# Sums of squared magnitudes taken on VectorE in every unit, with a new order of the work, in a gated-attention and feed-forward kernel

## The chip, the cores and the metric

The kernel runs on one core of a Trainium2 chip. The metric is the device time of one execution in microseconds; the median of three runs before the change is 659.39 (659.02 to 659.49). Engines are called as the profile calls them: PE (TensorE), PEld (its weight loads), DVE (VectorE), ACT (ScalarE), POOL (GpSimd) and SP (SyncE, which issues the DMAs here).

## The reference

For 4 batches and 8 heads, over 768 positions with head size 48, a complex gate decays a state, and the result goes through a feed-forward block:

```python
mag = np.sqrt(a_re * a_re + a_im * a_im)
scale = np.minimum(mag, 0.999) / (mag + 1e-06)
a_re_n, a_im_n = (a_re * scale, a_im * scale)
for t in range(S):
    new_re = ar * S_re - ai * S_im
    new_im = ar * S_im + ai * S_re
    S_re, S_im = (new_re + k[t] v[t]^T, new_im)
    y[t] = q[t] @ S_re
h = x @ w_in                      # x: y as 3072 tokens of 384; w_in 384 x 2048
sp = np.maximum(h, 0.0) + np.log1p(np.exp(-np.abs(h)))
g = h * erf(sp)
out = g @ w_out                   # 2048 x 384
```

(The state's update is written here in short; ar and ai are the scaled gates at t.)

## The kernel before

**Tiling.** The 3072 tokens are cut into 12 units `u` of 256 tokens, each of two chunks `c` of 128. Three units make up a batch. Within a chunk the recurrence is turned into matrix products: the logarithms of the gates' magnitudes and their angles are summed along time by products with a triangular matrix, keys and queries are multiplied with the decays and the sines and cosines, scores of 128 x 128 are masked, and a state of 96 x 48 per head is carried from chunk to chunk. The feed-forward part works on slabs of eight blocks of 128 columns.

**The order.** Every piece of work is a generator whose `yield`s cut it into steps of about one instruction (or one group of matmuls). A long string, `ORDER` (lines 49 to 168), lists 2,287 tokens; a loop (line 1391) takes them one after the other and runs the next step of the named piece. So `ORDER` fixes the order of instructions in the queue of each engine, SP's DMA queue among them. Each engine works its own queue in order and waits where an operand is not there.

The tokens that this document speaks of: `u` filler products on PE ahead of and between the first real ones; `g`, `k`, `q`, `v` loads; `n`, `i` weights' loads and their conversion, or a second look at them for the check; `m` squared magnitudes (lines 924 to 941), `t` the tangent, `l` logarithms, `r` arctangent, `a` angle sums, `s` sines, `p` decay sums; `K`, `Q` the scaled keys and queries, `A` scores, `S` state, `Y` the attention result; `h` the first feed-forward product, `x` softplus, `e` the erf and its four DVE steps, `f` sums, `O` the second feed-forward product (units 3 and up in seven half-size products, X, Y, Z and W, instead of eight); `Z` the end of the check. `e9.1.4` is unit 9, slab 1, blocks from 4.

**Table loads.** ACT's functions lie in three tables. The helper `act` (line 783) puts a table load in front of a function whose table is not the one loaded last, in the order of the program. Square lies in no table of the helper.

**The check.** The kernel computes by a shorter way that is valid for inputs in some bounds. It collects six sums, among them `large`, per row the sum of the squared magnitudes, compares their totals with limits, and stores one word, `ok` (line 1344). At the end every engine loads `ok` (line 1419) and branches (line 1420): were it 0, a general version of the kernel would follow; it is 1 here. Z has three steps: DVE sums up what was collected (lines 1333 to 1336), PE adds over the rows (line 1339), and DVE compares (lines 1343 and 1344).

**The lines that the change touches.** In unit 0, `g_mag` squares both gate parts on DVE and adds them with an instruction that also writes the row sum. In units 1 to 11 ACT does the squares, the first with the row sum as a second output, and DVE adds.

Of the kernel before, what the change touches and what calls it, by code (L numbers as in the profile page):

```python
# [17 lines left out]
OP = mybir.AluOpType  # L18
# [31 lines left out]
u8_0 u4_38 u4_21 u4_20 u4_2 g0.0 u2_34 u2_41 u2_25 g0.0 g0.1 g0.1 H t0.0 t0.0 m0.0 m0.0 m0.0 m0.1 t0.0 m0.1 l0.0  # L50
l0.0 t0.1 l0.0 l0.0 m0.1 l0.0 t0.1 t0.1 p0.0 u8_1 n0 n0 l0.1 o0.1 l0.1 l0.1 l0.1 o0.0 l0.1 n0 n0 k0.0 q0.0 p0.0
p0.0 K0.0 u2_23 r0.0 a0.0 r0.1 a0.0 a0.0 Q0.0 p0.1 u2_22 a0.1 u2_40 u2_39 g1.0 n1 m1.0 n1 n1 s0.0 s0.0 s0.0 Q0.0
qT0.0.0 p0.1 q0.1 a0.1 t1.0 p0.1 p0.0 K0.0 kT0.0.0 kT0.0.1 qT0.0.1 Q0.1 a0.1 t1.0 qT0.0.0 s0.1 s0.1 s0.1 qT0.0.1
g1.0 kT0.0.0 k0.1 u2_24 v0.0 S0.0 n1 K0.1 kT0.0.1 t1.0 o1.0 r1.0 A0.0.0 A0.0.0 Q0.1 K0.1 p0.0 S0.0 A0.0.1 A0.0.1
n3 n3 g1.1 m1.0 m1.1 t1.1 g1.1 a1.0 m1.0 a1.0 t1.1 a1.0 t1.1 qT0.1.0 qT0.1.0 v0.1 S0.1 S0.1 p0.1 l1.0 n4 n2 m1.1
m1.1 l1.0 g2.0 g2.0 p0.1 kT0.1.1 kT0.1.1 qT0.1.1 qT0.1.1 l1.0 o1.1 l1.0 n3 l1.0 Y0.0 kT0.1.0 A0.1.1 A0.1.1
kT0.1.0 A0.1.0 A0.1.0 l1.1 Y0.0 l1.1 s1.0 l1.1 n3 p1.0 p1.0 q1.0 l1.1 n2 l1.1 n2 g2.1 g2.1 p1.0 p1.0 n5 n6 r1.1
Y0.1 v2.1 k1.0 Y0.1 Q1.0 n2 n4 n4 n4 s1.0 s1.0 Q1.0 p1.1 a1.1 t2 m2 m2 m2 h0.0.6 t2 t2 S0.1 o2 n6 n6 p1.1 h0.0.6
l2 a1.1 a1.1 l2 p1.1 l2 l2 l2 K1.0 K1.0 n7 p1.1 q1.1 n6 k1.1 K1.1 Q1.1 g3.1 h0.0.4 h0.0.4 v1.0 a2.0 r2 a2.0 n7
n7 n7 n5 n5 qT1.0.1 qT1.0.0 h0.0.0 qT1.0.1 h0.0.0 s1.1 qT1.0.0 h0.0.2 h0.0.2 s1.1 s1.1 p2.0 p2.0 kT1.0.1 h0.1.0  # L60
kT1.0.1 kT1.0.0 a2.0 h0.1.0 kT1.0.0 p2.0 x0.0 a2.0 x0.0 e0.0.0 e0.0.2 A1.0.1 A1.0.1 A1.0.0 n5 n8 A1.0.0 n8 a2.0
S1.0 h0.1.6 h0.1.6 q2.0 p1.1 n9 K1.1 S1.0 n8 Q1.1 v1.1 a2.1 a2.1 Q2.0 n8 n9 p1.0 S1.0 Y1.0 Y1.0 qT1.1.1 qT1.1.1
qT1.1.0 qT1.1.0 a2.1 a2.1 a2.1 n9 kT1.1.1 kT1.1.0 n9 S1.1 S1.1 kT1.1.1 kT1.1.0 A1.1.0 A1.1.0 A1.1.1 s2 s2 s2
A1.1.1 S1.1 p2.1 p2.1 Q2.0 k2.0 g3.0 t3 p2.1 m3 t3 K2.0 Q2.0 K2.0 q2.1 Q2.1 K2.0 g3.1 g3.0 t3 v2.0 h0.1.4 Y1.1
Y1.1 n11 n11 k2.1 S2.0 h1.1.0 h0.1.4 m3 p2.0 o3 r3 h0.1.2 m3 l3 h1.1.0 l3 a3.0 a3.0 n10 l3 n11 S2.0 Q2.1 n11
K2.1 n10 l3 a3.0 l3 M2.0 M2.0 M2.0 M2.0 h0.1.2 K2.1 n10 K2.1 n10 g4.0 g4.1 a3.1 g4.1 g4.0 q3.1 h1.0.0 n12 x0.0
x0.0 e0.0.0 e0.0.2 a3.1 e0.0.2 h1.0.2 h1.0.2 p3.0 p3.0 p3.0 p3.1 p3.1 p3.1 k3.0 A2.0.0 e0.0.0 A2.0.1 A2.0.1
e0.0.0 e0.0.2 A2.0.0 e0.0.0 e0.0.2 Q2.1 h1.0.0 m4 a3.1 t4 a3.1 a3.1 m4 t4 e0.0.4 e0.0.4 n12 e0.0.4 t4 e0.0.6
e0.0.6 e0.0.4 e0.0.6 m4 e0.0.6 e0.0.4 n15 k3.1 h1.0.4 h1.0.4 s3 h1.0.6 h1.0.6 Y2.0 p2.0 q3.0 p3.1 n12 e0.0.6
S2.0 n12 M2.1 M2.1 M2.1 M2.1 n13 p3.0 v3.0 s3 p3.0 p3.1 s3 l4 x0.1 Y2.0 l4 x0.1 l4 x0.1 h1.1.6 h1.1.6 x0.1  # L70
e0.1.2 h1.1.2 e0.1.0 h1.1.2 Q3.0 n15 K3.0 Q3.0 l4 Q3.1 o4 n15 K3.0 r4 O0.1 O0.3 O0.0 O0.2 O0.4 O0.6 n15 K3.1
A2.1.0 A2.1.0 A2.1.1 A2.1.1 l4 e0.1.2 e0.1.0 e0.1.2 e0.1.0 h1.1.4 e0.1.2 e0.1.0 e0.1.2 e0.1.0 a4.0 a4.0 n14 Y2.1
v4.1 Y2.1 g5.0 e0.1.6 e0.1.6 e0.1.6 e0.1.4 e0.1.4 e0.1.4 n13 Q3.0 n13 p4.0 O0.5 O0.7 p4.0 a4.0 a4.0 p4.0 a4.0
e0.1.6 e0.1.4 n13 g5.0 a4.1 K3.0 n14 a4.1 e0.1.4 n14 e0.1.6 n14 x1.0 h1.1.4 x1.0 O0.8 h2.1.2 p4.1 O0.9 h2.0.2
O0.11 p4.1 x1.0 p4.1 x1.0 S3.0 S3.0 K3.1 g5.1 g5.1 M3.0 M3.0 M3.0 M3.0 e1.0.0 e1.0.0 e1.0.0 e1.0.2 e1.0.2 h2.0.2
e1.0.0 e1.0.2 e1.0.0 e1.0.2 e1.0.2 h2.1.2 m5 m5 a4.1 a4.1 j m5 O0.13 O0.15 O0.15 e1.0.4 h2.0.6 h2.0.6 e1.0.6
e1.0.6 e1.0.4 e1.0.4 e1.0.4 a4.1 e1.0.6 e1.0.6 e1.0.4 h2.1.4 A3.0.1 K3.1 A3.0.1 Q3.1 e1.0.6 Q3.1 v3.1 A3.0.0 l5
O0.10 A3.0.0 t5 l5 t5 x1.1 l5 l5 x1.1 S3.1 O0.12 O0.14 O0.14 x1.1 h2.0.4 O1.1 O1.3 h2.1.4 Y3.0 t5 S3.1 l5 o5
S3.1 x1.1 l5 l5 e1.1.2 e1.1.0 e1.1.2 e1.1.2 e1.1.2 e1.1.0 e1.1.0 e1.1.2 s4 s4 s4 r5 k4.0 K4.0 e1.1.0 e1.1.0 K4.0
e1.1.6 e1.1.6 e1.1.4 e1.1.4 e1.1.6 e1.1.4 e1.1.6 e1.1.6 O1.5 h2.0.0 O1.0 O1.2 M3.1 M3.1 M3.1 M3.1 A3.1.0 A3.1.0  # L80
A3.1.1 A3.1.1 O1.7 e1.1.4 K4.0 q4.0 Q4.0 k4.1 K4.1 e1.1.4 h2.0.0 h2.0.4 x2.0 Y3.0 x2.0 x2.0 x2.0 v4.0 p4.1 a5.0
p4.0 h2.1.6 O1.9 O1.11 S4.0 Y3.1 h2.1.0 O0.14 a5.0 K4.1 Q4.0 Q4.0 S4.0 q4.1 Q4.1 e2.0.0 e2.0.0 e2.0.0 e2.0.2
e2.0.2 e2.0.2 e2.0.0 e2.0.0 e2.0.2 p5.1 p5.1 h2.1.0 p5.1 e2.0.2 e2.0.6 Y3.1 h2.1.6 e2.0.6 e2.0.6 e2.0.4 a5.0
a5.0 e2.0.4 e2.0.4 O1.4 O1.6 O1.8 O1.13 O1.10 p5.0 p5.0 a5.0 a5.0 a5.0 x2.1 p5.0 x2.1 e2.0.4 e2.0.6 e2.0.6
h3.0.2 p4.0 M4.0 M4.0 M4.0 q5.1 M4.0 O0.15 k5.0 g6.1 p5.0 a5.1 g6.0 a5.1 a5.1 a5.1 x2.1 t6 x2.1 A4.0.1 A4.0.1
S4.1 S4.0 A4.0.0 A4.0.0 K4.1 S4.1 Q4.1 e2.0.4 Q4.1 e2.1.2 e2.1.2 e2.1.2 h3.0.4 h3.0.4 a5.1 O1.12 e2.1.0 e2.1.0
e2.1.2 a5.1 a5.1 e2.1.0 e2.1.2 e2.1.0 e2.1.0 p4.1 k5.1 g6.0 g6.1 h3.0.2 Y4.0 Y4.0 O1.14 O1.14 m6 m6 s5 e2.1.4
O1.15 O1.15 e2.1.6 e2.1.4 e2.1.6 e2.1.4 e2.1.6 h3.0.0 h3.0.0 s5 s5 e2.1.4 e2.1.4 S4.1 m6 e2.1.6 e2.1.6 h3.0.6
h3.0.6 M4.1 M4.1 M4.1 M4.1 h3.1.0 x3.0 t6 h3.1.0 x3.0 l6 x3.0 l6 x3.0 A4.1.1 h3.1.4 O2.1 O2.3 l6 K5.0 K5.0 q5.0
Q5.0 Q5.0 e3.0.0 Q5.0 v5.0 h3.1.6 A4.1.0 S5.0 t6 Q5.1 K5.1 A4.1.1 Q5.1 A4.1.0 Y4.1 K5.0 o6 S5.0 e3.0.0 e3.0.2  # L90
e3.0.0 e3.0.0 e3.0.2 e3.0.2 e3.0.0 e3.0.2 h3.1.4 r6 l6 O2.5 O2.7 a6.0 e3.0.6 a6.0 l6 e3.0.2 h3.1.2 O2.0 h3.1.2
h3.1.6 O2.9 e3.0.4 e3.0.6 e3.0.6 e3.0.4 a6.0 a6.0 O2.2 M5.0 a6.0 e3.0.4 M5.0 M5.0 M5.0 O2.4 O2.6 A5.0.0 A5.0.1
l6 l6 a6.1 p5.0 v6.0 q6.0 e3.0.6 e3.0.6 b2 e3.0.4 x3.1 Y4.1 h4.0.0 x3.1 a6.1 a6.1 x3.1 A5.0.0 A5.0.1 a6.1 a6.1
Y5.0 a6.1 b0 x3.1 O1.14 K5.1 K5.1 S5.0 a6.1 e3.0.4 Y5.0 f3.0 b4 Q5.1 e3.1.0 e3.1.0 e3.1.0 e3.1.0 e3.1.0 e3.1.2
e3.1.2 e3.1.2 e3.1.2 e3.1.2 k6.0 v6.1 O2.11 O2.13 p6.0 p6.0 p6.0 h4.0.0 p6.1 p6.1 e3.1.6 e3.1.6 h4.0.2 h4.0.2
e3.1.4 Q6.0 e3.1.4 O1.15 e3.1.4 e3.1.6 g7.0 g7.0 g7.1 p6.1 K6.0 f3.0 g7.1 m7 m7 M5.1 m7 e3.1.6 e3.1.4 e3.1.6
M5.1 i0 k6.1 i1 p6.0 q6.1 p6.1 M5.1 M5.1 O2.15 h4.0.4 h4.0.4 t7 O2.8 O2.10 O2.15 t7 l7 O2.12 O2.14 O2.14 O2.15
O2.14 b2 b2 t7 b0 b0 i0 l7 s6 l7 l7 b4 l7 b6 b2 e3.1.4 i1 f3.1 b6 b6 b4 h4.0.6 h4.0.6 x4.0 x4.0 b4 f3.1 l7 l7
x4.0 h4.1.0 O3.0 h4.1.0 x4.0 e4.0.0 a7.0 b6 O3.1 e4.0.2 h4.1.6 h4.1.6 o7 O3.1 r7 s6 A5.1.1 A5.1.1 O3.2 O3.2
e4.0.0 e4.0.2 e4.0.0 e4.0.2 e4.0.0 e4.0.2 e4.0.2 b0 e4.0.0 A5.1.0 s6 e4.0.4 e4.0.6 A5.1.0 a7.0 a7.0 e4.0.4  # L100
e4.0.4 e4.0.6 e4.0.6 h4.1.4 h4.1.4 O3.3 O3.4 h4.1.2 O3.5 v5.1 Y5.1 O3.6 O3.7 h4.1.2 x4.1 Y5.1 x4.1 a7.0 e4.0.4
Q6.0 Q6.0 K6.1 e4.0.6 O3.5 O3.5 K6.0 K6.0 O3.5 e4.0.4 Q6.1 O3.4 O3.7 O3.7 p6.1 M6.0 M6.0 e4.0.6 a7.0 a7.0 a7.0
x4.1 x4.1 e4.1.0 e4.1.0 e4.1.0 e4.1.2 p7.1 h5.0.2 h5.0.4 O3.8 O3.9 O3.12 p7.0 O3.10 O3.13 O3.11 p7.1 h5.0.2 p7.1
e4.1.2 e4.1.0 e4.1.2 e4.1.0 e4.1.2 e4.1.2 e4.1.6 e4.1.4 e4.1.6 e4.1.6 e4.1.4 e4.1.4 M6.0 M6.0 a7.1 g8.1 p6.0
a7.1 e4.1.6 e4.1.4 p7.0 h5.0.4 p7.0 a7.1 O3.13 e4.1.6 a7.1 f4.0 e4.1.4 f4.1 O3.11 S6.0 h5.0.6 g8.0 t8 t8 h5.0.6
m8 h5.0.0 Q6.1 i2 i2 A6.0.1 a7.1 a7.1 f4.1 a7.1 S6.0 q7.1 p7.0 i3 A6.0.1 O4.0 O4.1 A6.0.0 O4.2 O4.1 i3 O3.11
h5.0.0 A6.0.0 g8.0 O4.3 p7.1 g8.1 q7.0 O3.13 f4.0 O4.2 t8 o8 Q6.1 K6.1 K6.1 M6.1 M6.1 M6.1 x5.0 x5.0 x5.0 m8
x5.0 O4.4 O4.4 e5.0.2 e5.0.0 e5.0.2 e5.0.0 Q7.0 e5.0.2 e5.0.2 e5.0.0 m8 e5.0.0 e5.0.2 e5.0.0 h5.1.6 h5.1.6 s7 s7
s7 Q7.0 h5.1.2 h5.1.2 e5.0.6 e5.0.6 e5.0.4 e5.0.4 S6.1 e5.0.4 l8 M6.1 v7.0 O4.5 O4.5 S6.1 e5.0.6 h5.1.0 h5.1.4
h5.1.4 l8 h5.1.0 x5.1 Q7.1 S6.1 O4.5 e5.0.6 e5.0.4 O4.5 O4.6 O4.7 Y6.0 O4.7 O4.7 Q7.0 l8 l8 l8 A6.1.1 A6.1.1  # L110
x5.1 Y6.0 A6.1.0 O4.12 O4.13 A6.1.0 O4.8 Q7.1 k7.1 K7.1 v8.0 k7.0 K7.0 K7.0 K7.0 e5.0.4 e5.0.6 x5.1 l8 x5.1 l8
e5.1.0 e5.1.2 e5.1.0 e5.1.2 e5.1.0 e5.1.2 e5.1.0 e5.1.0 e5.1.2 e5.1.2 O4.9 Y6.1 Y6.1 O4.10 O4.11 p8.0 p8.0 p8.0
# [1339 lines left out]
```

## Time and profile before

| | |
|---|---|
| median of three runs | 659.39 us |
| the profiled execution | 659.63 us |
| its span, first to last instruction | 657.9 us |
| granted PE clock, mean | 0.997 |
| PE / PEld / DVE / ACT busy | 642.2 / 562.6 / 599.2 / 581.7 us |
| table loads on ACT | 95, 121.9 us |
| DMA | 70.19 MB, 107 GB/s on average |

In a row of groups, the parts are: line, engine, operation, output and inputs with their shapes, count, busy us and mean ns of one, and after the second bar how long the engine stood idle right before these instructions and what ended most of that. In the table of windows each row has the stretch, its length, then busy us and number of instructions of PE, PEld, DVE, ACT and POOL, the granted clock, the DMA share and GB/s. A row of waits names who waited, for whom, us in total, times, and the longest. The chain of waits is followed back from the last instruction; its rows are start, length and what ran. Matmul ends are modelled and matmuls overlap, so their busy time cannot show short gaps.

### The profile page before, as it was taken

The page shows a single profiled execution, that of the slowest core. Times are in us where ns is not written, and L with a number is a line of the kernel's source. Part 1 is how long each engine was busy: PE and PEld are TensorE (multiplying, and loading weights), DVE is VectorE, ACT ScalarE, POOL GpSimd, SP SyncE. Part 2 cuts the span into 40 slices and gives each one's busy share as a digit, 9 for nine tenths or more (in the row PEclk, how much of TensorE's full clock was granted, in tenths as well). Part 3 has the DMA queues.
Part 4 walks back from the last instruction along what each step waited for, and adds up shares of the span by engine and source line. Part 5 has one row for each costly group of instructions (what it writes and reads, how often), then busy time and mean ns, then how long its engine had stood idle before and what let it go on. Part 6 is the DMA issues. An engine that isn't in the chain of part 4 may idle for free.

```text
span 657.9 us, 12296 instructions
## 1 busy us (share of the span) xinstructions
PE 642.2 (98%) x4728; PEld 562.6 (86%) x4728; DVE 599.2 (91%) x976; ACT 581.7 (88%) x765; POOL 1.1 (0%) x8
## 2 busy tenths in 40 slices
PE   8999999999999999999999999999999999999995
PEld 7778887777777778989999998999998999999985
DVE  6999999999979899999999899899999998877883
ACT  6999999999999999998998999998996894788730
POOL 0000000000000000000000000000000000000000
PEclk9999999999999999999999999999999999999998
DMA  8896886536254358137448525626626507410020
GB/s 212 221 239 160 191 205 111 119 63 108 37 110 73 49 117 188 22 48 193 73 73 193 97 43 141 120 50 145 121 49 122 132 14 187 90 25 24 1 73 27
DMA packets 282792, 70.19 MB, mean 107 GB/s; under 512 B 269396, under 2 KB 272488, under 8 KB 282728
## 3 DMA queue, kind: packets, MB, share of 16 engines
q1 hardware_dynamic: 282728, 69.36, 49.0%
q8 instruction: 38, 0.62, 0.4%
q14 instruction: 26, 0.21, 0.1%
HBM read 48.82 MB, written 4.75 MB: 81 GB/s over the span
## 4 chain that ended last, share of the span: by engine, by line
PE 48%; ACT 30%; DVE 15%; DMA 3%; issue 3%; SPq 1%; POOL 0%; DVEq 0%; POOLq 0%; ACTq 0%
PE hps L1174 21%; ACT L787 7%; ACT yy L788 5%; ACT z L788 5%; PE Y L1267 4%; PE Z L1267 4%; PE X L1267 3%; PE y L1161 3%; PE sc L1106 3%; ACT e L788 3%; DVE z L1203 3%; DVE yy L1205 3%; DVE e L1207 2%; PE W L1267 2%; PE kv L1125 2%
## 5 line engine op out<-in xcount | busy, mean ns | idle before, releaser
L1174 PE MATMUL hps<-xT,w_in_sb 128*128 128x256 f32 x1152 | 260.7, 380 | 0.4 <-ACT xT L1163 0.3
L1174 PEld LDWEIGHTS hps<-xT,w_in_sb 128*128 128x128 f32 x1152 | 216.1, 190 | 32.6 <-ACT h L1177 1.4
L787 ACT ACT_TABLE_LOAD x95 | 121.9, 1283 | 2.4 <-PEq L1436 0.9
L1203 DVE TENSOR_TENSOR z<-z,yy 128x512 f32<-128x512 f32 x96 | 64.5, 687 | 18.6 <-ACT e L788 18.0
L788 ACT ACTIVATE e<-z 128x512 f32<-128x512 f32 x96 | 57.8, 627 | 21.1 <-DVE h L1209 20.6
L1209 DVE SCALAR_TENSOR_TENSOR h<-e,h 128x512 f32<-128x512 f32 x96 | 65.0, 685 | 1.3
L1243 PE MATMUL ops<-w_out_sb,h 128*128 128x384 f32 x192 | 66.2, 488 | 0.0
L1205 DVE SCALAR_TENSOR_TENSOR yy<-z,yy 128x512 f32<-128x512 f32 x96 | 64.6, 688 | 1.6
L1207 DVE TENSOR_TENSOR e<-e,yy 128x512 f32<-128x512 f32 x96 | 64.6, 685 | 0.9
L1177 ACT COPY h<-hps 128x512 f32<-128x512 f32 x96 | 54.5, 577 | 8.4 <-PE hps L1174 8.3
L1243 PEld LDWEIGHTS ops<-w_out_sb,h 128*128 128x128 f32 x192 | 35.8, 190 | 21.7 <-issue 0.8
L1106 PEld LDWEIGHTS sc<-KQ 96*128 96x128 f32 x384 | 47.0, 192 | 4.7 <-ACT KQ L1097 1.8
L1106 PE MATMUL sc<-KQ 96*128 96x128 f32 x384 | 49.0, 277 | 1.3 <-ACT KQ L1097 1.0
L788 ACT ACTIVATE yy<-z 128x2048 f32<-128x2048 f32 (+1 forms) x25 | 46.1, 1842 | 0.8 <-DVE found L859 0.4
L788 ACT ACTIVATE z<-h 128x2048 f32<-128x2048 f32 (+1 forms) x25 | 46.1, 1844 | 0.6 <-ACT h L1177 0.3
L788 ACT ACTIVATE z<-z 128x2048 f32<-128x2048 f32 (+1 forms) x25 | 46.1, 1845 | 0.5
L788 ACT ACTIVATE yy<-yy 128x2048 f32<-128x2048 f32 (+1 forms) x25 | 46.0, 1842 | 0.3
L1161 PE MATMUL y<-A,v 128*32 128x128 f32 x768 | 33.5, 275 | 0.9 <-DVE Skv L1131 0.6
L1110 DVE TENSOR_TENSOR A<-sc,triu 128x512 f32<-128x512 f32 x48 | 31.9, 679 | 1.8 <-PE sc L1106 1.8
L1125 PEld LDWEIGHTS kv<-v,kt 128*96 128x96 f32 x320 | 29.8, 165 | 1.6 <-issue 0.7
L1125 PE MATMUL kv<-v,kt 128*96 128x48 f32 x320 | 29.8, 246 | 0.0
L1267 PE MATMUL Y<-T,S 128*128 128x192 f32 x144 | 26.5, 331 | 1.5 <-DVE out L1275 1.1
(122 smaller groups left out, 1054.7 us busy)
## 6 DMA issues: line engine op xcount, KB each, us to landing
KQ<-X SPq DMA_DIRECT2D x240, 64.0 KB
raw<-in_moe_w_in_dram SPq DMA_DIRECT2D x8, 768.0 KB
raw<-in_moe_w_out_dram SPq DMA_DIRECT2D x8, 768.0 KB
again<-in_moe_w_in_dram SPq DMA_DIRECT2D x8, 768.0 KB
ar<-in_a_re_dram SPq DMA_DIRECT2D x24, 192.0 KB
ai<-in_a_im_dram SPq DMA_DIRECT2D x24, 192.0 KB
k<-in_k_dram SPq DMA_DIRECT2D x24, 192.0 KB
q<-in_q_dram SPq DMA_DIRECT2D x24, 192.0 KB
```

The costliest lines, as they stand in the source:

```text
L787: scalar.preload_act_table_set(sets[0])
L788: scalar.activation(func=func, **kw)
L1106: nc.tensor.matmul(out=ps[:, j, :], lhsT=head("k", g * HG + j, u, c), rhs=head("q", g * HG + j, u, c), start=True, stop=True)
L1125: nc.tensor.matmul(out=kv[0:D2, j, :], lhsT=T["kt", u, c][:, j].rearrange("p u d -> p (u d)"), rhs=side(T["v", u][:, c, j // 2], j % 2), s ...
L1174: nc.tensor.matmul(out=ps[:, e, :], lhsT=w_in_sb[:, (sl * SLAB + i) // 2, kd, e * P:(e + 1) * P], rhs=T["xT", u][:, kd, :], start=(kd == 0 ...
L1177: scalar.copy(out=T["h", u, sl][:, i:i + 2, :], in_=ps)
L1203: vector.tensor_tensor(out=z, in0=z, in1=y, op=OP.mult)
L1205: vector.scalar_tensor_tensor(out=y, in0=z, scalar=-2.0, in1=y, op0=OP.add, op1=OP.mult)
L1207: vector.tensor_tensor(out=e, in0=e, in1=y, op=OP.mult)
L1209: vector.scalar_tensor_tensor(out=h, in0=e, scalar=1.0 / RT2, in1=h, op0=OP.add, op1=OP.mult)
L1243: nc.tensor.matmul(out=ps, lhsT=lhsT, rhs=w_out_sb[:, i, :], start=i == HALF, stop=i == KF - 1)
L1267: nc.tensor.matmul(out=ps, lhsT=a(sl)[:, i], rhs=b(sl, i), start=sl == 0 and i == 0, stop=sl == NSL - 1 and i == HALF - 1)
```

## The change

`g_mag` becomes one form for all units: the squares stay where they were (DVE in unit 0, ACT in the others), ACT's first square gives no row sum any more, and the addition on DVE writes it in every unit. `large` so receives the sum of both squares; in units 1 to 11 it had that of the real part's. The whole of `ORDER` is replaced by another order of the same 2,287 tokens.

```diff
@@ g_mag
-        if u == 0:
-            for t, nm in ((s, "ar"), (y, "ai")):
+        for t, nm in ((s, "ar"), (y, "ai")):
+            if u == 0:
                 vector.tensor_tensor(out=t, in0=gate(nm, u, cc), in1=gate(nm, u, cc), op=OP.mult)
-                yield
-            vector.scalar_tensor_tensor(out=s, in0=s, scalar=1.0, in1=y, op0=OP.mult, op1=OP.add, accum_out=sums)
-            yield
-            return
-        act(out=s, in_=gate("ar", u, cc), func=AF.Square, accum_out=sums)
-        yield
-        act(out=y, in_=gate("ai", u, cc), func=AF.Square)
-        yield
-        vector.tensor_tensor(out=s, in0=s, in1=y, op=OP.add)
+            else:
+                act(out=t, in_=gate(nm, u, cc), func=AF.Square)
+            yield
+        vector.scalar_tensor_tensor(out=s, in0=s, scalar=1.0, in1=y, op0=OP.mult, op1=OP.add, accum_out=sums)
         yield
@@ ORDER, its first and its last lines
-u8_0 u4_38 u4_21 u4_20 u4_2 g0.0 u2_34 u2_41 u2_25 g0.0 g0.1 g0.1 H t0.0 t0.0 m0.0 m0.0 m0.0 m0.1 t0.0 m0.1 l0.0
-l0.0 t0.1 l0.0 l0.0 m0.1 l0.0 t0.1 t0.1 p0.0 u8_1 n0 n0 l0.1 o0.1 l0.1 l0.1 l0.1 o0.0 l0.1 n0 n0 k0.0 q0.0 p0.0
-p0.0 K0.0 u2_23 r0.0 a0.0 r0.1 a0.0 a0.0 Q0.0 p0.1 u2_22 a0.1 u2_40 u2_39 g1.0 n1 m1.0 n1 n1 s0.0 s0.0 s0.0 Q0.0
...
-O10.8 e11.1.0 e11.1.2 e11.1.0 e11.1.0 e11.1.2 e11.1.2 O10.9 O10.10 O10.11 O10.11 f11.0 f11.0 e11.1.6 e11.1.6
-e11.1.4 e11.1.4 O10.12 O10.13 O10.13 e11.1.6 O10.13 i15 O10.11 O11.0 O11.1 O11.3 e11.1.4 e11.1.6 e11.1.4 O11.1
-e11.1.4 e11.1.6 f11.1 f11.1 O11.4 O11.4 O11.2 O11.2 O11.6 O11.5 O11.7 O11.5 O11.5 O11.5 O11.7 i15 i15 Z O11.7
-O11.8 O11.9 O11.10 O11.11 O11.12 O11.11 O11.11 O11.13 O11.13 Z Z O11.13
+u4_38 u4_20 u4_21 u8_0 g0.0 g0.0 g0.1 g0.1 H t0.0 t0.0 t0.1 t0.1 m0.0 m0.0 t0.0 m0.0 l0.0 l0.0 l0.0 m0.1 m0.1 m0.1
+l0.1 l0.1 l0.1 u2_22 l0.0 l0.0 p0.0 p0.0 p0.0 u2_39 u8_1 o0.0 t0.1 o0.1 l0.1 l0.1 u2_25 r0.0 a0.0 r0.1 a0.0 n0
+n0 n0 n0 a0.0 s0.0 s0.0 s0.0 n1 n1 k0.0 K0.0 n1 q0.0 Q0.0 p0.1 u2_23 u2_34 u4_2 K0.0 a0.1 u2_24 kT0.0.1 u2_41
...
+O10.4 O10.5 e11.0.2 O10.5 e11.0.6 O10.7 O10.5 O10.7 O10.7 e11.1.2 e11.1.0 e11.1.0 e11.1.0 e11.1.0 e11.1.2
+e11.1.0 e11.1.2 h11.1.4 e11.1.2 e11.1.2 h11.1.4 x11.1.1 x11.1.1 x11.1.1 x11.1.1 O10.8 O10.9 O10.10 O10.11 O10.11
+f11.0 f11.0 O10.11 O10.12 O10.13 e11.1.6 Z Z O10.13 e11.1.4 O11.0 O10.13 e11.1.6 e11.1.4 e11.1.6 O11.1 O11.3
+e11.1.4 e11.1.6 O11.1 e11.1.4 e11.1.6 O11.4 e11.1.4 f11.1 O11.2 O11.6 O11.2 O11.5 Z O11.4 f11.1 O11.7 O11.5
+O11.5 O11.5 O11.7 O11.7 O11.8 O11.9 O11.10 O11.11 O11.11 O11.11 O11.12 O11.13 O11.13 O11.13
```

## The prediction

> **What bounds the kernel.** I read, in this order: the page's busy times, the table of windows, the groups by form, the waits, and the last microseconds. All numbers are of the profiled execution: its span is 657.9 us, its own time 659.63, and the median of the runs shown is 659.39, so 1.7 us lie around the span, and I take differences off the median.
>
> ```profile
> PE 642.2 (98%) x4728; PEld 562.6 (86%) x4728; DVE 599.2 (91%) x976; ACT 581.7 (88%) x765; POOL 1.1 (0%) x8
> ```
> ```profile
> core 0: us, PE busy (x) PEld busy (x) DVE busy (x) ACT busy (x) POOL busy (x), PEclk, DMA share, GB/s
> 0.00:40.00 40.00, 35.53 (x314) 29.89 (x315) 34.01 (x73) 34.12 (x66) 1.09 (x8) 1.00 0.87 215
> ...
> 117.00:210.00 93.00, 91.68 (x569) 70.07 (x569) 86.54 (x135) 91.26 (x120) 0.00 (x0) 1.00 0.48 89
> ...
> 300.00:402.00 102.00, 101.66 (x777) 94.03 (x776) 98.13 (x157) 96.87 (x118) 0.00 (x0) 1.00 0.52 109
> ...
> 500.00:606.00 106.00, 106.00 (x820) 98.32 (x819) 91.80 (x150) 81.93 (x96) 0.00 (x0) 1.00 0.38 86
> ...
> 637.00:658.00 21.00, 13.77 (x83) 13.03 (x82) 7.62 (x28) 0.00 (x0) 0.00 (x0) 0.91 0.07 23
> ```
> From 40 to 606 us PE is never out of work for long, while ACT and DVE are 90 to 98% busy up to 402 and slacker after. The waits view, asked for PE from 40 to 606 us, has seven waits, 2.7 us in all, the longest 0.9. So three engines are almost in balance and PE is a little the fullest. Time can be had in four places: the start, where PE has no real work until 10.38 us; PE's few dry spells; the last stage after 606, a chain through ACT, DVE and PE; and the 6.7 us between PE's last product (about 651.15) and the end of the span.
>
> **Part 1, the sums.** Units 1 to 11 take the sum from DVE's addition instead of ACT's first square. That is 12 instruction triples (unit 1 in two halves of 384 columns, ten units of 768).
>
> ```profile
> L940 DVE TENSOR_TENSOR s<-s,y 128x384 f32<-128x384 f32 x2 | 1.1, 554 | 0.2 <-ACT y L788 0.2
> L933 DVE SCALAR_TENSOR_TENSOR s<-s,y 128x384 f32<-128x384 f32 x2 | 1.1, 554 | 0.0
> L788 ACT ACTIVATION_READ_ACCUMULATOR s<-ar 128x1 f32 x12 | 2.4, 198 | 0.0
> L933 DVE DVE_READ_ACCUMULATOR s<-s,y 128x1 f32 x2 | 0.2, 82 | 0.0
> ```
> ACT loses 12 reads of 198 ns. In the timeline the next ACT instruction starts 0.09 us after such a read, so the engine gets back 12 x 0.09 = 1.1 us, at most 2.4. DVE's new form costs what the old one did: 554 ns both, at the same shape. Its reads (82 ns) start together with the next instruction (5.83 and 5.83 us), so 12 of them cost between 0 and 1.0 us; I take 0. The Trainium skill speaks against this edit: "Vector Engine (DVE) Microarchitecture Reference", under "Points that are easy to get wrong", says that this kind of DVE instruction runs at half throughput when both sources lie in SBUF and are not bf16, because no read port is left for the accumulator. By that rule the additions would grow by their own start-to-start distance, 10 x 0.87 + 2 x 0.48 = 9.7 us of DVE. The L933 row has exactly this case, fp32 from SBUF with an accumulator, and shows no doubling; I follow the row.
>
> **Part 2, table loads.** `act` issues a load where the table differs from that of the last table function. Walking the old ORDER by this rule gives 95 loads, the x95 of the page's L787 row (121.9 us, 1283 ns each); the new one gives 93. That is -2.6 us of ACT. Up to the first gelu of unit 7 (the load at 414.8 us now) the new order has 63 against 68, so ACT is 5 x 1.28 = 6.4 us less loaded where it is fullest; three of the five come back in units 8 and 9, where ACT has slack. None of this is time by itself, since PE's work is unchanged: it can only remove dry spells. Bounds for 40 to 606 us: the new order moves each PE step by 2.7 places on average (18 at most), DVE's by 4.5, so new dry spells can come as well. Best, the 2.7 us of waits and about 1.3 of small gaps go, -4; worst, as many again come, +4. I take -0.9: ACT's 3.7 us of relief (1.1 + 2.6), of which about a quarter reaches PE, as PE is the fuller engine. SP's own moves are part of that range: loads of v sit farther ahead of their use (median 131 steps of ORDER against 45), which helps against the 2.5 us "DMA v" pieces in the chain of waits at 117.5 and 233.7; the row-into-column loads of w sit nearer (20 against 30).
>
> **Part 3, the start.** Before the first product (p0.0) the old order has 30 filler products, 60 records that took 8.96 us (0.149 each); the new one has 22. p0.0 started at 10.28, right behind the fillers and without a wait, though its operand was there at 8.44 + 0.55 = 8.99. With 16 records less, the fillers end near 7.9 and the operand decides. The new ACT order runs t0.1 ahead of l0.0, which by my sum of the rows (seven ACT instructions of 0.45 after the gates land, then DVE's last step) leaves the operand at about 8.8. So p0.0 starts some 1.4 us sooner. ACT, which waited 1.2 us for it, follows, and unit 1's square (0.5 us) no longer stands ahead of s0.0. Against it: the loads n1 (768 KB) go out ahead of k0.0 and q0.0. At the 212 GB/s of the first slice that is 3.7 us more ahead of them, which puts q near 15 us; it was used at 16.1. I estimate that half or more of it is hidden. Sum: -0.8, between -1.9 and +2.
>
> **Part 4, the last stage.** DVE work of the kernel's self-check (i15 and the first step of Z) is moved. i15's two reductions (1.0 us) go ahead to where DVE waits on PE anyway. Z's first step (about 0.7 us) goes in front of the last erf steps, where the chain of waits runs through DVE (z at 630.92 to h at 636.7). What hides it: ACT reaches the last gelu about 0.35 us earlier, since h11.1.4's copy no longer delays x11.1.0, and O11.1's and O10.13's DVE steps shift by as much. Z's product now stands in PE's queue ahead of O11.0, so PE waits there if Z's sums are late; PE has 1.8 us of waits between 631 and 638 to absorb it. Bounds -0.8 to +1.5; I take -0.4.
>
> **Part 5, the end.** Now the check's result is the last DVE work, after the last output, and every engine waits for it before it may branch.
>
> ```profile
> 651.18 0.36 DVE out L1275
> 651.54 0.39 DVE within L1343 x6
> 651.93 0.02 issue
> 651.96 0.15 DVE ok L1344
> ```
> ```profile
> L1420 POOLq COMPARE_BRANCH  x1: 59/59/59, 653.0 to 653.0; - x1
> ...
> L1420 SPq COMPARE_BRANCH  x1: 70/70/70, 653.3 to 653.3; - x1
> ...
> L1420 POOLq EVENT_SEMAPHORE  x1: 17/17/17, 657.0 to 657.0; - x1
> ```
> ```profile
> SPq L1447 <- POOLq L1420: 2.1, 1, 2.1
> ```
> POOL needs 4.0 us from its branch to its next instruction, and SP, done itself at 654.9, waits 2.1 us for it. In the new order Z ends before O11.5's reads, some 10 us earlier. POOL has no other work, so it branches then and its 4 us lie beside PE's last products. SP branches after the last output is issued (651.57 + 0.33 = 651.90) instead of at 652.1. That is 2.1 + 0.2 = 2.3 us off the end. "Runtime: NRT & Kernel Launch", section "Instruction fetch mechanics", has the general rule: a taken branch out of the fetched window stalls its engine until a fetch is done. Taken for all engines, SP, PE and DVE, which still branch after 651.9, would each stall about 4 us as well and nothing would be won. The rows limit it to POOL: SP goes from 653.3 to 653.8, DVE from 653.1 to 653.7. By the row -2.3, by the rule 0; I take the row.
>
> Sum: -2.3 - 0.4 - 0.8 - 0.9 = -4.4, so 659.4 - 4.4 = **655.0 us**.
>
> **Rivals.** (a) Only the end is won, and start, middle and last stage even out: 659.4 - 2.3 = 657.1, chance 0.20. For it: PE's queue was nearly full already. (b) All of PE's dry spells and the better start come through: -2.3 - 0.8 - 1.9 - 3 = -8, 651.4, chance 0.15. (c) No change: POOL's stall stays at the end, or the end's 2.3 us are given back by as much stalling; 659, chance 0.09. (d) Slower: a late small DMA holds a DVE step, DVE's queue stands behind it, and PE runs dry. The chain of waits has such pieces, 2.2 us for w at 163.5, 4.0 for s at 184.9, 4.6 for k at 251.5. Each new one in the balanced stretch up to 402 us costs about 2.2; two pay back the 4.4, from the third on it is slower. Three to four: +2.2 to +4.4, 662. For it: w's shorter lead; against it: v's longer lead and ACT's relief. Chance 0.13. The forecast itself has 0.43.
>
> The range takes in (a), (b) and the forecast with the bounds of parts 2 to 4: 651.0 to 660.3. Faster by over 0.2% (1.3 us, about what a measurement of this kernel can tell from no change) is forecast, (a) and (b): 0.78. Same 0.09, slower 0.13.
>
> **What would show it.** Table loads x93; no ACT read on s<-ar and 12 more DVE reads, with the L933 group at 768 columns near 950 ns, not 1.8 us. POOL's event long before the end and no SP wait on POOL. p0.0 near 9 us. PE waits from 40 to 606 us at or under 3 us. I am wrong if POOL's stall stays at the end, if PE's waits in the middle exceed 6 us, or if DVE's wait for the k, q or w loads in the first 100 us grows by more than 2 us.

## The result and the profile after

| | before | after |
|---|---|---|
| median, 20 runs each | 659.48 us | 658.09 us |
| lowest to highest | 658.47 to 660.67 | 657.34 to 658.88 |
| profiled execution, its span | 659.63, 657.9 | 657.62, 655.8 |

The ratio is 0.9979, with a 95% interval of 0.9973 to 0.9986: the change gains 1.4 us where 4.4 were forecast. The direction was right, and the time lies in the range.

First the busy times of the changed kernel, from its page:

```profile
PE 643.6 (98%) x4728; PEld 563.3 (86%) x4728; DVE 599.0 (91%) x988; ACT 579.3 (88%) x751; POOL 1.1 (0%) x8
```

ACT has lost 2.4 us of work and 14 instructions, DVE has gained 12 instructions and no time. The table of windows of the changed kernel, with the columns of before:

```profile
0.00:40.00 40.00, 36.75 (x318) 31.65 (x319) 34.86 (x77) 34.63 (x65) 1.09 (x8) 1.00 0.86 213
...
300.00:402.00 102.00, 100.21 (x772) 92.35 (x772) 97.32 (x157) 94.76 (x114) 0.00 (x0) 1.00 0.54 111
...
500.00:606.00 106.00, 105.87 (x825) 97.84 (x824) 93.66 (x151) 79.65 (x94) 0.00 (x0) 1.00 0.40 91
...
637.00:658.00 21.00, 14.09 (x83) 13.03 (x81) 6.86 (x19) 0.00 (x0) 0.00 (x0) 0.95 0.06 21
```

In the first slice PE does more than before (36.75 against 35.53 us, four records more). From 300 to 402 it does less (100.21 against 101.66). ACT has 2.1 us less to do there, and PE has not got it. In the last slice DVE has nine instructions fewer: the end of the check has left it.

The parts of the change show in the groups by form of the changed kernel:

```profile
L787 ACT ACT_TABLE_LOAD x93 | 119.3, 1283 | 2.4 <-PEq L1431 0.9
...
L935 DVE SCALAR_TENSOR_TENSOR s<-s,y 128x768 f32<-128x768 f32 x10 | 9.5, 948 | 0.1
...
L935 DVE SCALAR_TENSOR_TENSOR s<-s,y 128x384 f32<-128x384 f32 x4 | 2.2, 552 | 0.0
...
L935 DVE DVE_READ_ACCUMULATOR s<-s,y 128x1 f32 x14 | 1.1, 82 | 0.0
```

There are 93 table loads, as counted. The addition with an accumulator takes 948 ns at 768 columns and 552 at 384 (the plain addition took 554). And the end, from the instructions of the branch's line:

```profile
L1415 POOLq COMPARE_BRANCH  x1: 59/59/59, 641.8 to 641.8; - x1
...
L1415 POOLq EVENT_SEMAPHORE  x1: 17/17/17, 644.7 to 644.7; - x1
...
L1415 SPq COMPARE_BRANCH  x1: 70/70/70, 652.9 to 652.9; - x1
```

POOL branches at 641.8 and is back at 644.7, while PE's last product starts only at 651.7. Nobody waits for POOL any more.

The middle shows little in the view that the prediction used. The waits of PE from 40 to 606 us, in the kernel before:

```profile
PE sum L921 <- ACT xT L1163: 0.9, 1, 0.9
PE y L1161 <- DVE Skv L1131: 0.6, 1, 0.6
...
```

and in the changed kernel:

```profile
PE hps L1169 <- ACT xT L1158: 0.8, 1, 0.8
PE sum L921 <- ACT xT L1158: 0.6, 2, 0.3
PE hps L1169 <- ACT h L1172: 0.5, 1, 0.5
PE sc L1101 <- DMA w<-wrow: 0.5, 1, 0.5
PE sum L1012 <- ACT xT L1158: 0.3, 1, 0.3
```

In the changed kernel they are 2.7 us in all, the same as before. **So I measured PE's progress instead.** Each matmul gets the typical distance from one of its form to the next instruction, and I compare the times at which two kernels have done equal amounts. The mean of four traces with the old order outside Z (before, sums_only, free_end_old, late_product) against that of four with the new one (after, order_only, end_undone, free_end_new):

| old order's time, us | 43 | 125 | 288 | 321 | 448 | 567 | 613 | last product |
|---|---|---|---|---|---|---|---|---|
| new order later by, us | -0.7 | +0.3 | -1.7 | -0.2 | -0.4 | +1.4 | +1.3 | +1.0 |

Taken only at points where both orders have done the same products, the same traces give this picture within 0.3 us; between such points the orders have done different products, and a single column (321 above all) can be off by half a us. At 613 us the four new traces lie from 0.6 to 2.0, the four old ones within 0.6 of each other. So the start gains 0.7, the middle loses 2.0, the last stage gains 0.4. From the start of PE's last product to the end of the span it takes 5.8 to 6.8 us where Z ends last (before, sums_only, end_undone, copies_down; mean 6.35), and 4.04 to 4.13 in the fifteen traces with Z early: a gain of 2.3. The sum is -0.7 + 2.0 - 0.4 - 2.3 = -1.4, the measured change.

### The profile page after: what moved, and what is told of

Same layout as the page of the kernel before. It is cut to its first block, busy times and chain, and to the rows that moved or that the text cites. A ratio compares the mean times of both kernels' runs of the same rounds, so it can differ in the third digit from the quotient of the medians.

```text
span 655.8 us, 12318 instructions
## 1 busy us (share of the span) xinstructions
PE 643.6 (98%) x4728; PEld 563.3 (86%) x4728; DVE 599.0 (91%) x988; ACT 579.3 (88%) x751; POOL 1.1 (0%) x8
## 4 chain that ended last, share of the span: by engine, by line
ACT 48%; PE 26%; DVE 15%; issue 4%; DMA 3%; SPq 2%; POOL 0%; DVEq 0%; ACTq 0%; POOLq 0%
PE hps L1169 10%; ACT L787 10%; ACT yy L788 9%; ACT z L788 9%; ACT e L788 4%; ACT h L1172 3%; PE Y L1262 3%; PE X L1262 3%; ACT CS L788 2%; ACT th L788 2%; DVE yy L1200 2%; ACT y L788 2%; DVE z L1198 2%; DMA q<-in_q_dram 2%; ACT s L788 2%
## 5 line engine op out<-in xcount | busy, mean ns | idle before, releaser
L788 ACT ACTIVATE pr<-sum 128x384 f32<-128x384 f32 x48 | 21.9, 492 | 6.5 <-PE sum L922 5.1
```

The costliest lines, as they stand in the source:

```text
L788: scalar.activation(func=func, **kw)
```

## The experiments

All medians are in us, with the number of runs; ratios are to the kernel before, run beside it on the same chip (659.27 to 659.58), each with its 95% interval. A token's step is counted from 0: `Z[1]` is Z's product.

### Sums, order and end apart

**sums_only** and **order_only** take one half of the change each: the new `g_mag` in the old order, and the old `g_mag` in the new order.

> The new g_mag in the old order. My theory: no change that can be told, 659.2 to 659.5 (ACT gives back 1.1 us that is mostly idle time then). Rival: the sums themselves cost the time that is missing from my sum, DVE's 12 additions with reads push back a full DVE: 660.5 to 661.

> The new order with the old g_mag. My theory: as the new kernel within 0.4 us, 658.1 to 658.5. Rival, that the order was fitted to the sums on DVE and that these bring the gain: 659.5 or more; and if the sums cost time: 656.7.

Measured: sums_only 658.84 (13), 0.9999 (0.9990 to 1.0007); order_only 658.35 (13), 0.9991 (0.9983 to 0.9999). The sums do nothing that can be seen, although they take reads off ACT. What the change gains is in the order, as far as this tells: order_only alone gains 0.9 us by the medians (0.6 by its ratio) and the whole change 1.4, and their intervals overlap.

**end_undone** is the changed kernel with Z back at the old end, and **end_only** the old kernel with Z behind f11.0 and i15 some 100 tokens earlier:

```diff
 end_undone
-... f11.0 f11.0 O10.11 O10.12 O10.13 e11.1.6 Z Z O10.13 ... O11.2 O11.5 Z O11.4 ... O11.7 O11.7 O11.8 ... O11.13 O11.13
+... f11.0 f11.0 O10.11 O10.12 O10.13 e11.1.6 O10.13 ... O11.2 O11.5 O11.4 ... O11.7 Z O11.7 O11.8 ... O11.13 Z Z O11.13
 end_only
-... f11.0 f11.0 e11.1.6 ... O11.4 O11.4 ... O11.7 i15 i15 Z O11.7 ... O11.13 O11.13 Z Z O11.13
+... f11.0 f11.0 Z Z e11.1.6 ... O11.4 Z O11.4 ... O11.7 O11.7 ... O11.13 O11.13 O11.13
```

> The new kernel with Z's three steps put back to the end. My theory: POOL's 4 us are on the path again, so 2.3 to 2.8 us more than the new kernel, 660.4 to 660.9, which is slower than the old kernel: the rest of the new order is worse than the old one by 1 to 1.5 us. Rival, that the rest of the order is what gained: 658 to 659.

> The old kernel, old sums and old order, in which only the self-check's end stands where the new order has it (i15 earlier, Z's first two steps behind f11.0, its third ahead of O11.4's DVE step). My theory: the end alone is worth what the two profiles show between PE's last product and the span's end, 6.8 against 4.0 us, so 2.8 us: 656.7. Rival A, that the end is worth nothing by itself and the gain comes from elsewhere in the order: 659.5. Rival B, that Z's new place delays the last stage by as much as it wins: 658 to 659.

Measured: end_undone 660.34 (11), 1.0022 (1.0012 to 1.0031), so without the end's gain the new kernel is slower than the old one, and the end is worth 660.34 - 658.09 = 2.25 us (2.8 by the two ratios, each taken beside the kernel before). end_only 661.47 (5), 1.0035 (1.0022 to 1.0049): a miss of mine. One of its waits from 620 to 660 us, and two of its windows, say why:

```profile
PEld all L1333 <- DVE sums L1330: 4.3, 1, 4.3
```
```profile
628.40:630.80 2.40, 0.04 (x1) 0.00 (x0) 2.37 (x5) 2.35 (x4) 0.00 (x0) 1.00 0.00 0
630.90:637.60 6.70, 5.19 (x18) 5.16 (x19) 2.62 (x12) 1.42 (x3) 0.00 (x0) 0.50 0.00 0
```

In the old order Z's product then stands ahead of products that were ready (in the changed kernel O10.12 and a step of O10.13 come before it), and PE waits 4.3 us for DVE's sums. Late in this wait the granted clock, the column after POOL, falls to 0.50, and it stays there until 637.7. PE is busy for 5.19 us of that at half speed, which I estimate at another 2.6 us. The place was wrong, not the idea.

**free_end_old, free_end_new, late_product, new_end** search for the free place. Z's sums go behind O11.7's third step, and the product into a gap of PE's queue. In late_product and new_end it stands one product later. The old kernel is the base of free_end_old and late_product, the changed one of the others.

```diff
 free_end_old
-... i15 i15 Z O11.7 O11.8 O11.9 O11.10 O11.11 O11.12 O11.11 O11.11 O11.13 O11.13 Z Z O11.13
+... i15 i15 O11.7 Z O11.8 Z O11.9 O11.10 O11.11 O11.12 Z O11.11 O11.11 O11.13 O11.13 O11.13
 late_product
+... i15 i15 O11.7 Z O11.8 O11.9 Z O11.10 O11.11 O11.12 Z O11.11 O11.11 O11.13 O11.13 O11.13
```

> The old kernel, only Z's product between O11.8 and O11.9 and its compare ahead of O11.11's DVE step, where DVE waits on PE anyway; nothing else is moved. The earlier run put Z's product two products too early in PE's queue, where it held PE for 4.1 us. My theory: a freed end is worth the full difference of the tails, 2.8 to 2.9 us: 656.5. Rival, that an early end gives only what end_undone against the new kernel shows, about 2.2: 657.1. If the end is worth nothing by itself: 659.3.

> The new kernel with Z at the same free place instead of in front of the last erf steps. My theory: Z's sums and PE's wait for them (0.9 us at 630.8) cost the last stage little or nothing, since PE waits there again for DVE at 637: 657.4 to 658.1. Rival, that Z's early place costs the last stage the 0.9 us: 657.2.

> The kernel before with its own order everywhere but for Z: the check's six sums behind the third step of O11.7, its product on PE ahead of the product of O11.10, one product later than in free_end_old, the comparison ahead of the first sum of O11.11. If PE's wait for the sums (0.94 us in free_end_old) is all that was lost there, and the branch of POOL is still hidden: 657.73 - 0.9 = 656.8, and lower than the changed kernel by about 1.3. If the ok word now comes too late, so that POOL's stall shows behind the last output again: 658 to 659.

> The changed kernel with Z at the place of late_product (sums behind the third step of O11.7, product ahead of O11.10's, comparison ahead of O11.11's first sum), nothing else: so it differs from new_start only in the order of work between PE's 20th and last microsecond, and has the same sums and the same end. By the milestones of PE (start -0.86, middle +2.2, last stage -0.35 against the order of before): late_product's 656.75 + 1.0 = 657.7, and 1.6 above new_start. If the middle of the new order costs nothing and the milestones deceive: 656.0 to 656.5.

| | median (n) | ratio, interval |
|---|---|---|
| free_end_old | 657.73 (21) | 0.9978 (0.9972 to 0.9985) |
| late_product | 656.75 (6) | 0.9956 (0.9941 to 0.9972) |
| free_end_new | 658.30 (21) | 0.9983 (0.9977 to 0.9990) |
| new_end | 658.60 (14) | 0.9989 (0.9981 to 0.9998) |

Waits of PEld from 625 to 660 us, free_end_old:

```profile
PEld Y L1261 <- DVE out L1269: 1.4, 1, 1.4
PEld all L1333 <- DVE sums L1330: 1.2, 1, 1.2
```

and late_product:

```profile
PEld Y L1261 <- DVE out L1269: 1.4, 1, 1.4
...
PEld all L1333 <- issue: 0.2, 1, 0.2
```

Only the wait for the sums is gone, and 0.98 us with it. **late_product beats both kernels**: the old order with three tokens moved. In the new order the same move does not help. The changed kernel's PE waits 1.0 us for Z's sums too; in new_end that is gone, and a wait of 1.2 us for DVE's S has come.

### Where the new order loses

**new_start** has the new sums, the new order for PE's first 20 us of work (up to about 43 us) and the old order after it, with late_product's end. new_end differs from it in the order after that point, with Z at the same place.

> The changed kernel's sums, its order of work up to where PE has done 20 us of work, the order of before from there on, and Z as in late_product. By the sum of parts: 656.8 (late_product) less the 0.86 us that the new order had gained by 44 us = 655.9. If the seam between the two orders costs as in the two other mixed orders (2.2 to 2.5 us), or the lead is lost until 127 us as in the changed kernel: 657 to 658.5.

Measured: 656.06 (6), 0.9945 (0.9930 to 0.9960). From late_product it can't be told apart, the intervals overlap; in its trace PE waits 1.6 us for the operand of p0.0, the lead is only 0.2 us at 43 us, and it is gone at 65. Against new_end it is 2.5 us faster (2.9 by the ratios), with intervals far apart. **So the new order behind the start costs about 2.5 us**: the loss that the milestones show is real.

**new_to_400, new_but_c and new_to_295** follow the new order up to 447, 447 and 295 us and the old one after that. new_but_c also has the old order from 44 to 127 us.

> New sums; the new order up to about 447 us, the old order for all that is left, Z at the free place. Three traces of each order put the new one 1.0 us ahead at this point and 0.8 us behind at 626 us. My theory: the stage from 447 to 530 us is what loses, so this is the free end's time with the old order less 1.0: 655.5. Rival, that the lead is lost whatever order follows, because another engine sets the pace of the later stage: 656.5, as with the old order throughout.

> As new_to_400, but with the old order from about 44 to 127 us, where the traces put the new order's second loss (0.9 us). My theory: a lead of 1.0 from the start plus 0.9 from 127 to 447 us: 654.7. Rival, that a lead of the start cannot be kept through the stage up to 127 us, in which the weights' loads and ACT set the pace: 655.5 as new_to_400.

> The changed kernel's sums and its order of work up to 295 us, the order of before from there on, Z as in late_product. By the milestones the new order leads by 1.7 us there, and everything that it loses comes later: 656.75 - 1.7 = 655.0, the fastest so far. If the lead is given back at the seam, or wherever ACT and DVE catch up: 656.5 to 657.5.

Measured: 660.34 (21), 1.0018 (1.0011 to 1.0026); 660.13 (20), 1.0013 (1.0006 to 1.0020); 659.54 (14), 1.0005 (0.9996 to 1.0015). All three miss. By PE's milestones the first two lose 2.2 to 2.5 us and the third 3.9 within 30 us of the seam, where, I take it, steps that one order had put off fall due at once. Up to the seam the first two move as the order that they follow, and the third does so from 43 us on. Its trace had lost 2.4 us before that: PE waited 2.2 us for its first real product, until 10.6 us, and the granted clock was 0.50 from 11.8 to 15.2 us. The nine of its runs with a mean clock of 0.999 or more have a median of 659.15, which misses too. For the question asked the three are inconclusive.

### Late copies of h?

Between 40 and 606 us one row of PEld's waits had grown, from the first of these rows (before) to the second (changed):

```profile
PEld hps L1174 <- ACT h L1177: 1.1, 4, 0.4
```
```profile
PEld hps L1169 <- ACT h L1172: 4.0, 13, 0.8
```

ACT's copies of h free the two buffers that the products of h fill, and in the new order they stand behind table loads and halves of e. My theory was that this is the loss. **copies_up** moves seven of them up in the changed kernel; **copies_down** moves four of them down in the old one.

```diff
 copies_up, one of seven
-p7.0 e4.1.4 O3.12 O3.13 p7.1 e4.1.4 e4.1.4 e4.1.6 e4.1.6 e4.1.6 e4.1.6 e4.1.6 h5.0.4 O3.10
+p7.0 h5.0.4 e4.1.4 O3.12 O3.13 p7.1 e4.1.4 e4.1.4 e4.1.6 e4.1.6 e4.1.6 e4.1.6 e4.1.6 O3.10
 copies_down, one of four
-O3.0 h4.1.0 x4.0
+O3.0 x4.0 h4.1.0
```

> The changed kernel with seven of ACT's copies of h (of h1.0.6, h2.1.4, h4.1.4, h5.0.4, h5.0.0, h8.0.6, h9.0.0) moved ahead of the ACT steps that stand directly before them and that nothing near waits for, nothing else changed. Theory (the middle lost its gain because PE waits for copies that free ps_h's two buffers): PE's waits for `ACT h` fall from 4.0 us to about 2, the seven products start on time, and the time falls by 1 to 2 us against the changed kernel, to 656 to 657. Rival (those waits are only where an unavoidable lag of PE shows itself, since PE catches up or waits somewhere else): the waits of these seven go, others of the same size come, 657.8 to 658.4.

> The kernel before, with four copies of h put behind the ACT step that followed them: h0.1.2 behind one of 1.93 us (its slack was 0.31), h1.0.0 behind two of together 1.77 (slack 0.12), h1.1.4 behind one of 1.94 (slack 0.98), h4.1.0 behind one of 1.91 (slack 0.93). The lateness so made is 1.6 + 1.65 + 0.95 + 1.0 = 5.2 us. Theory (PE has no reserve in the middle, a late copy reaches the end one for one): 659.4 + 4 to 5.2 = 663.4 to 664.6, with PE's waits for `ACT h` up from 1.1 by about 5. Rival (the steps moved ahead of the copies give part of it back, or PE makes it up in a wait that it had anyway): under 661.5.

copies_up: 658.07 (15), 0.9976 (0.9968 to 0.9984), no gain on the changed kernel. Its PEld waits from 40 to 606 us:

```profile
PEld sum L915 <- ACT xT L1152: 1.5, 2, 1.0
PEld hps L1163 <- ACT h L1166: 1.4, 5, 0.5
PEld hps L1163 <- ACT xT L1152: 1.3, 1, 1.3
...
PEld Y L1256 <- DVE S L1209: 0.8, 1, 0.8
```

The waits for copies fell from 4.0 to 1.4 us as meant, and a new wait for S is there. At 302 us PE had waited 0.58 us for a copy; now it starts that product on time and waits 0.69 at 306 us for S. DVE's timeline there, in copies_up:

```profile
303.91 0.95 DVE L853 TENSOR_REDUCE found<-again 128x1 f32<-128x768 f32 x1
304.79 0.67 DVE L1198 SCALAR_TENSOR_TENSOR h<-e,h 128x512 f32<-128x512 f32 x1
305.39 0.96 DVE L1064 STREAM_TRANSPOSE X<-kt 128x768 f32<-128x768 f32 x1
306.28 0.64 DVE L1209 TENSOR_TENSOR S<-h 128x512 f32<-128x512 f32 x1
```

DVE has no idle time there, and S stands behind a maximum for the check and a transpose. In the changed kernel S runs at the same time (306.27): ACT's late copy had hidden DVE's late S. It is the same at 454 us (ACT's split of a10.0 instead of a copy, 0.5 us) and at 530 us (a transfer, 0.81 instead of 0.29).

copies_down: 661.75 (9), 1.0034 (1.0023 to 1.0046), or +2.3 us for 5.2 us of lateness. The 1.5 us wait at 85 us and the 1.0 at 129 stay in PE's milestones; the 1.15 at 270 is given back within 50 us. About half reaches the end, between both expectations.

**followers_up** also moves what came late behind the copies:

```diff
-Q6.1 K6.1 i2 i2 e4.1.4 K6.1 f4.1 i3
+Q6.1 K6.1 i2 e4.1.4 f4.1 i2 K6.1 i3
 (and p10.0 behind a10.0, h9.0.6 ahead of r11.0, Q10.1 ahead of O8.2, i11 behind it)
```

> copies_up (the changed kernel with seven copies of h moved up) and, in the places where its trace shows PE waiting for something else a few products later, that too moved up: at 305 us DVE's S of f4.1 ahead of a maximum and a transpose (PE waited 0.69 us for it), at 454 us ACT's split of a10.0 ahead of two steps of p10.0 (0.5 us), at 498 us the copy of h9.0.6 ahead of a table load and a tangent (0.3 us), at 530 us DVE's transpose of Q10.1 ahead of a sum that still waits and of a maximum, so that the transfers of its rows start earlier (0.81 us). Theory (each of these places has two or three inputs that come late together, and the gain shows only when the last of them comes earlier): up to 2.3 us less than copies_up's 658.07, 656 to 657. Rival (PE is held by the total of ACT's and DVE's work there, so that a third input is late by as much): 657.6 to 658.3.

Measured: 665.50 (6), 1.0088 (1.0069 to 1.0107), far outside both. The wait at 306 us is gone, but at 321 us PE waits 0.9 us for a copy of h, and at 340 us 2.1 for xT, where copies_up waited 1.15. At 459 us it waits 1.4 us for `pr`, a result of p10.0, which this experiment itself had put back: ACT computes it at 459.4, in copies_up at 453.8. There the experiment made its own dry spell and does not test its theory. Both longer waits are followed by a lower clock. The windows of followers_up:

```profile
337.00:341.00 4.00, 2.51 (x16) 2.21 (x14) 3.00 (x5) 3.94 (x6) 0.00 (x0) 1.00 0.17 26
342.10:345.50 3.40, 3.40 (x10) 2.69 (x9) 3.33 (x6) 3.36 (x4) 0.00 (x0) 0.50 0.52 81
456.00:461.00 5.00, 3.61 (x21) 2.73 (x19) 3.88 (x8) 3.42 (x8) 0.00 (x0) 1.00 0.86 265
461.60:465.00 3.40, 3.40 (x16) 3.22 (x16) 3.40 (x6) 2.23 (x4) 0.00 (x0) 0.50 0.70 169
```

The granted clock is 0.50 for 3.4 us behind each wait, while PE is busy, so by estimate another 3.4 us are lost beside the waits. The one of the six runs with a mean clock of 1.000 took 662.85 us, the others 664.77 to 665.99. From 530 to 563 us PE also waits 3.0 us where copies_up waited 0.8; the cause of that was not looked for.

**xt_up and xt_copies_up** take the longest single wait of the middle away, for xT of Y6.1 at 338 us, from the changed kernel and from copies_up:

```diff
-a8.0 e5.1.0 Q7.1 e5.1.0 e5.1.0 e5.1.0 Y6.1 e5.1.2
+a8.0 Y6.1 e5.1.0 Q7.1 e5.1.0 e5.1.0 e5.1.0 e5.1.2
```

> The changed kernel with one of ACT's copies moved: xT of Y6.1, which at 338 us lets PE wait 0.99 us (its longest wait in the middle), goes ahead of the table load and the half of e that stand before it, 1.9 us earlier; its product has ended by then. If PE is held there by this one place in ACT's queue: 658.1 - 1.0 = 657.1, and the wait is gone. If PE then waits for another late input a few products on, as in copies_up: 657.8 to 658.3.

> copies_up with the same copy of xT moved up. In copies_up this wait had grown from 0.99 to 1.15 us, so it may be the place that took back what the seven copies of h had gained by 321 us. If so: 658.07 - 1.15 = 656.9 or a little less. If the middle takes it back again before 570 us: 657.8 to 658.3.

Measured: 658.55 (21), 0.9987 (0.9981 to 0.9994), and 658.86 (22), 0.9987 (0.9981 to 0.9993): nothing gained. The 0.99 us at 338 is gone in both. In xt_up PE waits at 345, 350 and 351 us instead, 0.29 + 0.70 + 0.33, ahead of a product of h, a product of a sum along time and a score; one of these appears in its waits of PE from 340 to 352 us:

```profile
PE sum L916 <- DVE parts L999: 0.4, 1, 0.4
```

In copies_up at 302 us, in xt_up and in xt_copies_up a wait was removed, and each time the next input was late by about as much.

## Why the prediction was right and wrong

**Part 1, the sums: right.** They were put at about nothing, and sums_only shows 0.9999. DVE's form costs what the row said. By the rule of the Trainium skill ("Vector Engine (DVE) Microarchitecture Reference", "Points that are easy to get wrong") DVE would have grown by 9.7 us, by the prediction's estimate; its busy time fell by 0.2, so this case does not show the rule.

**Part 3, the start: right in size.** -0.8 forecast, -0.7 at 43 us, and the later loads did not eat the gain: DVE waits 2.5 us for loads in the first 100 us, 3.1 before. The step to it was not as forecast. p0.0 starts at 9.40, not near 9: its operand was there at 8.86, as forecast, but the 44 filler records, forecast to end near 7.9, still ran until 9.3. In six other traces of the new start the last filler begins between 7.9 and 8.6, and PE waits 0.5 to 0.9 us for the operand. As a single edit the start was not isolated: in new_start the lead was gone behind the seam.

**Part 4, the last stage: right, as far as the traces tell.** -0.4 forecast, -0.4 by the milestones (-0.3 between the changed kernel with order_only and the kernel before with sums_only, the pairs that differ in Z's whole move), with PE's wait for Z's sums (1.0 us) inside the 1.8 that were there to absorb it.

**Part 5, the end: right.** -2.3 forecast, -2.3 by the tails, -2.25 by end_undone. Of the two prices weighed there, the row held. The rule ("Runtime: NRT & Kernel Launch", "Instruction fetch mechanics"), read as 4 us for every engine, did not. SP, PE and DVE branch after 649 us, and the longest from a branch to the next event of these three is PE's (649.6 to 652.1), beside its last products. What ends last now is the last output: issued at 652.5, landed at 654.4 by SP's wait for it.

**Part 2, the middle: this step failed**: "I take -0.9: ACT's 3.7 us of relief (1.1 + 2.6), of which about a quarter reaches PE". Measured are +2.0 us by the milestones and about +2.5 by new_end against new_start. Three things were wrong in it.

- The relief was smaller. ACT's busy time fell by 2.4 us, not 3.7: the sums alone gave 1.2 (sums_only), as forecast, but the order alone 1.1 (order_only), although its two loads fewer are 2.6.
- The quarter was a guess without a row. Relief of ACT can reach PE only where PE waits for ACT. In sums_only the relief was worth nothing measurable, and in the changed kernel ACT does 2.4 us less and PE is later.
- A cost was bounded (+4 for new dry spells) but not charged. In the new order copies of h and xT, which PE waits for, stand behind table loads and halves of e, and PEld's waits for copies of h went from 1.1 to 4.0 us. The forecast counted ACT's load and never looked which of its steps moved back. That these copies are what costs the time is not shown: moving them forward again gained nothing.

Of the loss, about +1.0 us arises between 43 and 125 us, +1.5 between 288 and 350, and +1.7 between 448 and 567. A gain of 2.0 lies between 125 and 288. From 44 to 625 us the matmuls' distances beyond the typical one grew, in the same two sets of traces, from 8.9 to 10.0 us where a gap is over 0.12 us, and by 0.9 in all the shorter ones together, so nearly half of it stands in gaps too short for the view of waits. It is not PE's own sequence of forms: with the typical distance taken for each pair of forms, the short gaps grow as well, by 1.3 us. **What stays open** is the cause: the late copies and the longest wait were each tried and do not give the time back, and the try on the copies' followers spoiled itself in one of its four places. That ACT's and DVE's work together holds PE there fits copies_up and the two runs with xT, but it was only argued. It wasn't tried to lighten both in the same stage.

The shape of the result was that of rival (a), "only the end is won", with 0.9 us less: its "start, middle and last stage even out" came as -0.7, +2.0 and -0.4.

## What to carry to other kernels

- Where three engines are about 90% busy or more, a busy time that falls on a feeding engine need not be time won: look at the steps the fullest engine waits for and see whether they moved forward or back. And removing one wait was worth only the distance to the next late input here.
- Work whose result every engine needs at the end (a status word, a branch) belongs in front of the last products, at a place where the fullest engine need not wait for it. Three moved tokens were worth 2.7 us here (late_product), about twice what the whole change brought; end_only, with the wrong place, lost 2.2.
- When waits look the same in two traces, compare when each has done equal work; it finds a loss that is spread over many gaps too short for a row.

## What the hardware showed unexpectedly

- PE's sequencer runs ahead of the work that it has queued: in the changed kernel it branches at 649.6, while products run on whose last starts at 651.7. From the instructions of the branch's line and from PE's timeline:

```profile
L1415 PEldq COMPARE_BRANCH  x1: 393/393/393, 649.6 to 649.6; - x1
```
```profile
649.30 2.76 PE L1262 MATMUL W<-w_out_sb,h 128*128 128x192 f32 x16
```

- SP loads `ok` at 641.3 us, ahead of its own output transfers at 650.1 and 652.5. In its trace the wait for the first of these outputs follows the load (642.1), so the load may simply stand earlier in SP's queue; that it overtook them is not shown.
- POOL's stall behind its branch is not fixed: 4.0 us before, 2.8 in the changed kernel.
- The granted clock can halve behind a short wait of PE. It was 0.50 for 3.4 us behind waits of 2.1 and 1.4 us in followers_up and of 2.2 us at 10.6 us in new_to_295, and 0.50 for 6.8 us in end_only, where PE waited 4 us. It stayed at 1.00 behind a wait of 2.2 us at 313 us in new_to_295 and of 1.5 us at 85 us in copies_down. What decides it is open.
